# Output matmuls as four 32-row float32 strips, two batches at a time, in place of split fp32r products

## The chip, the cores and the metric

The kernel runs on one core of a Trainium2 chip. The metric is the device time of one execution in microseconds. The profiled execution is one execution of its own, recorded on the chip; its span is the time from its first to its last instruction.

## The reference

Three layers follow one another. Attention between 512 tokens and 32 state slots gives, for each of B = 8 batches, 544 rows of 512 numbers. A dense layer with a clipped square as its activation follows (w_in 512 x 2048, w_out 2048 x 512). The third layer is a soft mixture of experts, and the code that changes is its end:

```
logits = x @ phi                                  # 4352 tokens x 32 slots
d = softmax over tokens;  slot_input = d.T @ x    # 32 x 512
for e in range(8):                                # 4 slots per expert
    slot_out[e] = relu(slot_input[e] @ w1[e]) @ w2[e]
c = softmax over the 32 slots
out = c @ slot_out                                # 4352 x 32 times 32 x 512
```

Everything is float32. The output is 4352 x 512 numbers, 8.91 MB.

## The kernel before

The batches b = 0 to 7 (512 tokens each) and then one batch of the 256 state rows (b = B = 8) run through attention, the dense layer and the running softmax over tokens. What follows after that, in the profile from 455 us, is the tail. In it the slot inputs are multiplied by w1 (L906, sixteen slices of 1 MB), turned (L932) into `hTD`, and multiplied by w2 (L950, tile `SO`, again sixteen slices). All w1 and w2 slices are loaded by SyncE's queue (some by GpSimd's) as SBUF places come free (`give`, `take`, `free`).

The logits of every token lie in `LT` (and `LTs` for the state rows), transposed: 32t to 32t+31 are the 32 slots of the t-th 128 tokens of a batch, so `LT[32t:32t+32, 128b:128b+128]` is what the output matmul of 128 tokens needs as its stationary operand. `csoft` makes the softmax over slots in place, in VectorE and GpSimd, by way of the place `ct`.

The output matmul before the change works in fp32r, a float32 form whose matmul takes one record where float32 takes two. To keep the precision, each factor is split into a rounded part and the remainder. `csplit` brings the four strips of `LT` into one strip by multiplying with 0/1 matrices `pick` (tile `cX`), and writes rounded part and remainder under one another into `LC` (two batches per tile, `LCs` for the state rows). `slot_out(dh)` makes the slot outputs of one column half (dh = 0 or 1, 256 columns): eight steps of eight `SO` matmuls, one w2 slice each, then an eviction to `SOs`, a matmul with `R` that repeats the 32 rows four times (`SR`), and evictions into the four tiles `so`, whose unused rows are zeroed beforehand. `combine(dh)` makes the output of a column half: per 128 tokens two fp32r matmuls into `ops` (128x256), an eviction by VectorE or ScalarE in turn, and per batch one transfer of 512 KB from SyncE's queue. The state rows take eight transfers of 32 KB from GpSimd's queue per half.

Both are generators: the letters of `CFG["so"]` say whose turn it is, s for a step of `slot_out(1)`, c for a step of `combine(0)`. After that come what is left of both, and `combine(1)`. The build reorders instructions on an engine within their dependences, by a model of its own, so the order on an engine needn't be the order of the code.

```
    s1, c0 = slot_out(1), combine(0)
    for x in CFG["so"]:
        step(s1 if x == "s" else c0)
    drain(s1)
    drain(c0)
    drain(combine(1))
```

Of the kernel before, what the change touches and what calls it, by code (L numbers as in the profile page):

```python
# [7 lines left out]
F32 = mybir.dt.float32  # L8
# [8 lines left out]
CFG = dict(hp=2000, att7=(3, 5, 6, 7, 8, 10), og=1, n3=1, n3m=10, wS=['DP', 'AD', 'AD', 'AD', 'AD', 'DP', 'AD', 'DD', 'AD', 'AD', 'AD', 'AD', 'AD', 'AD', 'AD', 'AD'], xsm=13, k0=5, rg=6, spg=0, att0=6, att=7, V0=(2, 6, 10), Vn=(0, 4, 10), Vx=12, wn='H', wsev='adad', conv=(4, 8, 9, 11, 12, 13, 19, 21, 24, 26, 28, 32, 36, 40, 44, 48, 52, 56, 60), todo=[1, 1, 1, 2, 0, 0, 0, 3, 0, 0, 2, 2, 1, 1, 0, 0], E0=2, E=1, sm=1, tqB=(5, 9, 13), GP=10, pe=(3,), psH=3, gtpX=(0, 7), tq0=(13, 15), keep=(2, 3, 4, 5), x2=(1, 1), natm=1, warm=14, bounce7=(0, 3), split=1, wt=4, so='ssccsccccccsss', smm=(1, 2, 3, 4, 5, 6, 9), tqv=(), tqvm=0, first='x', apath=2, f32c=1, place=1, attm=(3, 6, 7, 8, 9, 12), subPm=True, loDm=False, bounce=(0, 1, 2, 3), bq=('s', 's'), xq='s', nat=((1, 11), (2, 2), (2, 3), (2, 11), (3, 2), (3, 4), (3, 9), (4, 2), (4, 3), (4, 9), (5, 2), (5, 3), (5, 9), (6, 2), (6, 4), (6, 9)), subP=(1,), mulD=(), loD=(), qlag=0, gv0='EEEEEEEEEEEEEEEE', gv='EEEEEEEEEEEEEEEE', gvS='BBBBBBBBBBBBBBBB')  # L17
# [3 lines left out]
def kernel(  # L21
# [657 lines left out]
    def csplit(parts, C):  # L679

        np_ = 64 * len(parts)
        X = psX.tile([128, 512], F32, tag="X", name="cX")[0:np_, 0:C.shape[1]]
        for q, (L, n) in enumerate(parts):
            for t in range(n // 128):
                mm(out=X[64 * q:64 * q + 64, 128 * t:128 * t + 128], lhsT=pick[0:n // 4, t, :], rhs=L, start=True, stop=True)
        act(C, X)
        for p in range(32, np_, 64):
            nc.vector.tensor_tensor(out=C[p:p + 32], in0=X[p:p + 32], in1=C[p:p + 32], op=ALU.subtract)

# [212 lines left out]
    for i in range(16):  # L902
        e, hf = divmod(i, 2)
        place, w = where["w1", i]
        for kt in range(4):
            mm(out=h1[hf][32 * kt:32 * kt + 32, :], lhsT=XD[e // 4][:, kt, 32 * (e % 4):32 * (e % 4) + 32], rhs=w[kt],  # L906
               start=(e == 0), stop=(e == 7))
        if i >= CFG["k0"] and len(place) == 1 and got < 4:
            got += 1
            kept.append(place)  # L910
        else:
            give(place)
# [3 lines left out]
    pick = tail4[:, 1, 0:2].rearrange("p a (b x) -> p (a b) x", b=2)  # L916
    for t in range(4):
        nc.vector.tensor_scalar(out=pick[:, t, :], in0=R[:, 0:64], scalar1=blk[:, t:t + 1], scalar2=None, op0=ALU.mult)
# [3 lines left out]
    LC = take(kept.pop(0), "LC", F32R)[1]  # L922
    LCs = const.tile([64, 256], F32R, tag="wp", name="LCs")
# [12 lines left out]
    so = take(kept.pop(0), "so", F32R)[1]  # L936
    for t in so:
        nc.vector.tensor_scalar(out=t.rearrange("p (a b) -> p a b", a=2),
                                in0=cst_t[:, 0:256].unsqueeze(1).to_broadcast([128, 2, 256]),
                                scalar1=0.0, scalar2=None, op0=ALU.mult)  # L940
    so = [so[0:2], so[2:4]]

    def slot_out(dh):
# [14 lines left out]
        for q in range(2):  # L958
            p, p2 = slice(64 * q, 64 * q + 64), slice(64 * q, 64 * q + 32)
            act(so[0][q][p, dc], SR[p])  # L960
            nc.vector.tensor_tensor(out=so[1][q][p2, dc], in0=SR[p2], in1=so[0][q][p2, dc], op=ALU.subtract)

    def combine(dh):
        dc = slice(256 * dh, 256 * dh + 256)
        n_ev = 0
        for b in list(range(B - 2)) + [B, B - 2, B - 1]:
            T = ntok(b) // 128
            place = next(p for p in free if p[0][2] >= 256 * T)
            free.remove(place)
            o = take(place, "o")[0][0][:, 0:256 * T].rearrange("p (t d) -> p t d", t=T)  # L970
            for t in range(T):
                q, p, L = (b % 2, slice(0, 128), LC[b // 2]) if b < B else (0, slice(0, 64), LCs)
                ps = (psH, psX)[n_ev % 2].tile([128, 256], F32, tag="HX"[n_ev % 2], name="ops")
                for i in range(2):
                    mm(out=ps, lhsT=L[p, 128 * t:128 * t + 128], rhs=so[i][q][p, dc], start=(i == 0), stop=(i == 1))  # L975
                if n_ev % 2:
                    act(o[:, t, :], ps)
                else:
                    nc.vector.tensor_copy(out=o[:, t, :], in_=ps)  # L979
                n_ev += 1  # L980
            if b < B:
                dma(out=out[544 * b:544 * b + 512, dc].rearrange("(t p) d -> p t d", p=128), in_=o)
            else:
                for bb in range(B):
                    t, q = divmod(bb, 4)
                    (nc.gpsimd.dma_start if CFG["og"] else dma)(out=out[544 * bb + 512:544 * bb + 544, dc], in_=o[32 * q:32 * q + 32, t, :])  # L986
# [4 lines left out]
    csplit([(LTs, NS)], LCs)  # L991
# [47 lines left out]
```

## Time and profile before

| | us |
|---|---|
| median of 3 runs | 539.94 |
| the runs | 536.88, 539.94, 543.04 |
| profiled execution: its span, the only time recorded of it | 537.7 |
| TensorE busy in it (matmul) | 481.8 (90%) |
| VectorE busy | 395.4 (74%) |
| ScalarE busy | 256.0 (48%) |
| GpSimd busy | 239.8 (45%) |

The share of TensorE is an average over stages with different limits; the rows further down keep the stages of the tail apart. DMA share is the mean busy share of the 16 DMA engines; about 1 means that they had no more to give.

### The profile page before, as it was taken

The page shows a single profiled execution, that of the slowest core. Times are in us where ns is not written, and L with a number is a line of the kernel's source. Part 1 is how long each engine was busy: PE and PEld are TensorE (multiplying, and loading weights), DVE is VectorE, ACT ScalarE, POOL GpSimd, SP SyncE. Part 2 cuts the span into 40 slices and gives each one's busy share as a digit, 9 for nine tenths or more (in the row PEclk, how much of TensorE's full clock was granted, in tenths as well). Part 3 has the DMA queues.
Part 4 walks back from the last instruction along what each step waited for, and adds up shares of the span by engine and source line. Part 5 has one row for each costly group of instructions (what it writes and reads, how often), then busy time and mean ns, then how long its engine had stood idle before and what let it go on. Part 6 is the DMA issues. An engine that isn't in the chain of part 4 may idle for free.

```text
span 537.7 us, 9910 instructions
## 1 busy us (share of the span) xinstructions
PE 481.8 (90%) x3757; PEld 273.0 (51%) x3757; DVE 395.4 (74%) x728; ACT 256.0 (48%) x508; POOL 239.8 (45%) x230
## 2 busy tenths in 40 slices
PE   4476999999987999999999999999997997999992
PEld 2132455665534555455455455456466683356481
DVE  2999989777578679969969979977964762345260
ACT  2343476576555456456455455455444462023152
POOL 0775667665317366465555555646471000110032
PEclk9686799999999999999999999999998999899996
DMA  8998082457378488789789878879797988996379
GB/s 314 419 402 325 1 293 100 157 177 197 117 227 322 110 296 289 240 251 276 283 219 274 276 222 265 285 221 349 260 324 217 364 338 306 388 419 249 118 254 294
DMA packets 40223, 140.30 MB, mean 261 GB/s; under 512 B 4336, under 2 KB 12912, under 8 KB 28272
## 3 DMA queue, kind: packets, MB, share of 16 engines
q1 hardware_dynamic: 38496, 131.81, 71.2%
q0 software_dynamic: 1680, 7.87, 4.4%
q8 instruction: 29, 0.48, 0.3%
q14 instruction: 18, 0.15, 0.1%
HBM read 98.24 MB, written 39.32 MB: 256 GB/s over the span
## 4 chain that ended last, share of the span: by engine, by line
PE 60%; DVE 18%; DMA 13%; ACT 3%; issue 2%; SPq 2%; POOL 0%; POOLq 0%; DVEq 0%; ACTq 0%
PE h L434 22%; PE F L123 5%; DMA gdr<-gD 4%; PE E L123 4%; PE V L123 4%; PE SO L950 4%; DMA nat<-gD 4%; PE h L442 4%; DMA nat<-gdr 3%; PE ops L975 3%; PE h L906 3%; DVE win L160 3%; PE gtp L512 2%; DVE win L158 2%; DVE v L384 2%
## 5 line engine op out<-in xcount | busy, mean ns | idle before, releaser
L434 PE MATMUL h<-a,v 128*128 128x512 f32 x744 | 200.3, 412 | 5.0 <-DVE nat L486 2.2
L464 POOL TENSOR_TENSOR c<-c 128x512 f32<-128x512 f32 x128 | 135.6, 1064 | 100.4 <-ACT c L132 99.9
L434 PEld LDWEIGHTS h<-a,v 128*128 128x128 f32 x744 | 133.9, 191 | 85.1 <-issue 28.2
L132 ACT ACTIVATE c<-h,half 128x512 f32<-128x512 f32 x128 | 87.8, 688 | 99.1 <-PE h L434 66.6
L486 DVE SCALAR_TENSOR_TENSOR g<-h,c 128x512 f32<-128x512 f32 x112 | 75.2, 672 | 29.8 <-POOL c L464 29.7
L521 DVE STREAM_TRANSPOSE gD<-g 128x512 f32<-128x512 f32 x108 | 75.6, 703 | 1.6
L132 ACT ACTIVATE v<-V 128x512 fp32r<-128x512 f32 x62 | 37.0, 597 | 29.5 <-DVE v L384 14.8
L384 DVE TENSOR_TENSOR v<-V,v 128x512 fp32r<-128x512 f32 x62 | 42.1, 679 | 10.5 <-ACT v L132 9.7
L123 PE MATMUL V<-win,st_t 64*32 64x512 f32 x64 | 35.1, 629 | 9.8 <-POOL win L168 6.5
L128 PE MATMUL V<-win,st_t 64*32 64x512 f32 x448 | 38.3, 630 | 0.0
L123 PE MATMUL F<-nat,dN 128*32 128x512 f32 x54 | 26.9, 601 | 4.5 <-DMA nat<-gdr 2.9
L123 PE MATMUL E<-g,wp 128*32 128x512 f32 x56 | 29.2, 604 | 0.7 <-DVE g L486 0.7
L128 PE MATMUL E<-g,wp 128*32 128x512 f32 x168 | 29.6, 604 | 0.0
L128 PE MATMUL F<-nat,dN 128*32 128x512 f32 x162 | 27.2, 601 | 0.0
L986 POOL DMA_DIRECT2D out_dram<-o x16 | 7.9, 501 | 42.8 <-DVE o L979 37.2
L442 PE MATMUL h<-XSh,v 128*128 128x256 f32 x128 | 26.4, 298 | 0.2 <-ACT nat L132 0.2
L979 DVE COPY o<-ops 128x256 f32<-128x256 f32 x34 | 13.6, 423 | 15.8 <-PE ops L975 15.4
L623 DVE SCALAR_TENSOR_TENSOR acc<-acc,al,F 128x512 f32<-128x512 f32 x28 | 20.7, 739 | 5.7 <-PE F L128 5.5
L320 POOL TENSOR_TENSOR a<-att,a 128x512 fp32r<-128x512 f32 x14 | 18.1, 1305 | 13.4 <-ACT a L132 13.4
L975 PE MATMUL ops<-so,LC 128*128 128x256 f32 x128 | 23.3, 308 | 0.2
L442 PEld LDWEIGHTS h<-XSh,v 128*128 128x128 f32 x128 | 21.2, 197 | 4.1 <-issue 1.9
L264 POOL TENSOR_TENSOR att<-att,m 128x512 f32<-128x512 f32 x14 | 15.1, 1081 | 18.3 <-DVE m L263 15.6
(239 smaller groups left out, 780.9 us busy)
## 6 DMA issues: line engine op xcount, KB each, us to landing
gdr<-gD SPq DMA_DIRECT2D x100, 256.0 KB, 4.8
nat<-gdr SPq DMA_DIRECT2D x25, 1024.0 KB, 5.5
w<-in_w_dram SPq DMA_DIRECT2D x24, 1024.0 KB, 8.8
xn<-in_xn_dram SPq DMA_DIRECT2D x8, 1024.0 KB, 7.7
out_dram<-o SPq DMA_DIRECT2D x16, 512.0 KB, 5.4
xs<-in_xs_dram SPq DMA_DIRECT2D x7, 1024.0 KB, 7.7
w<-in_w_dram POOLq DMA_DIRECT2D x5, 1024.0 KB, 9.5
wb<-in_win_dram SPq DMA_DIRECT2D x4, 1024.0 KB, 11.7
```

Of the source, the lines that this page charges most:

```text
L123: first = mm(**calls[0])
L128: e = mm(**c)
L132: return nc.scalar.activation(out=out, in_=in_, func=func, **kw)
L384: nc.vector.tensor_tensor(out=lo[:, G, :], in0=V[G], in1=hi[:, G, :], op=ALU.subtract)
L434: mm(out=h, lhsT=v[:, G, f], rhs=a[:, G, :], start=(k == 0), stop=(k == 5))
L442: mm(out=h, lhsT=w[:, j, :], rhs=x[:, j, :], start=(k == 0), stop=(k == 11))
L464: nc.gpsimd.tensor_tensor(out=c, in0=c, in1=c, op=ALU.mult)
L486: gI[b, m] = nc.vector.scalar_tensor_tensor(out=g, in0=h, scalar=1.0, in1=c, op0=ALU.max, op1=ALU.min)
L521: nc.vector.transpose(out=gd[:, :, :, m4, :].rearrange("p c a i -> p a c i"), in_=gT[b, m].rearrange("p (a c i) -> p a c i", a=4, i=32))
L623: nc.vector.scalar_tensor_tensor(out=a, in0=a, scalar=al, in1=F, op0=ALU.mult, op1=ALU.add)
L950: mm(out=SO[c:c + 32, :], lhsT=hTD[:, ft, 32 * e:32 * e + 32], rhs=w[ft // 2][:, 256 * (ft % 2):256 * (ft % 2) + 256], start=(e == 0 and f ...
L975: mm(out=ps, lhsT=L[p, 128 * t:128 * t + 128], rhs=so[i][q][p, dc], start=(i == 0), stop=(i == 1))
```

## The change

`csplit`, `pick`, `LC`, `LCs` and the zeroed `so` tiles are gone; two SBUF places fewer are set aside for them. `so` is now one float32 piece of the tile `tail` (128x512), which holds the 32 slot outputs four times under one another, as `SR` delivers them: one eviction of 128x256 per half. The output matmul takes strip t of `LT` as it lies, with 32 rows, and strip t of `so`, in float32. The helper `group` issues the matmuls of the four strips next to one another and keeps them together by a priority.

`combine` now goes through five groups per half: batches 0 and 1, then the state rows, then 2 and 3, 4 and 5, 6 and 7. Strip t has a PSUM bank of its own (`banks`): two banks of the pool V and two of X, or three of H and one of X, in turn. In a bank the two batches stand side by side, so that one eviction takes 128x512. The transfers per batch are those of before. `CFG["so"]` changes from `ssccsccccccsss` to `cscscscscssss`: each group of `combine(0)` is followed by one step of `slot_out(1)`, and four steps are left at the end.

```diff
...
-    def csplit(parts, C):
-
-        np_ = 64 * len(parts)
-        X = psX.tile([128, 512], F32, tag="X", name="cX")[0:np_, 0:C.shape[1]]
-        for q, (L, n) in enumerate(parts):
-            for t in range(n // 128):
-                mm(out=X[64 * q:64 * q + 64, 128 * t:128 * t + 128], lhsT=pick[0:n // 4, t, :], rhs=L, start=True, stop=True)
-        act(C, X)
-        for p in range(32, np_, 64):
-            nc.vector.tensor_tensor(out=C[p:p + 32], in0=X[p:p + 32], in1=C[p:p + 32], op=ALU.subtract)
-
...
         for kt in range(4):
             mm(out=h1[hf][32 * kt:32 * kt + 32, :], lhsT=XD[e // 4][:, kt, 32 * (e % 4):32 * (e % 4) + 32], rhs=w[kt],
                start=(e == 0), stop=(e == 7))
-        if i >= CFG["k0"] and len(place) == 1 and got < 4:
+        if i >= CFG["k0"] and len(place) == 1 and got < 2:
             got += 1
             kept.append(place)
         else:
...
 
     ct_place = kept.pop(0)
     ct, = take(ct_place, "ct")[0]
-    pick = tail4[:, 1, 0:2].rearrange("p a (b x) -> p (a b) x", b=2)
-    for t in range(4):
-        nc.vector.tensor_scalar(out=pick[:, t, :], in0=R[:, 0:64], scalar1=blk[:, t:t + 1], scalar2=None, op0=ALU.mult)
     csoft(LTs, 128, 64, SIs)
     csoft(LT, 128 * B, 128, ct)
     free.append(ct_place)
-    LC = take(kept.pop(0), "LC", F32R)[1]
-    LCs = const.tile([64, 256], F32R, tag="wp", name="LCs")
     hTD_t, = take(kept.pop(0), "hTD")[0]
...
-    so = take(kept.pop(0), "so", F32R)[1]
-    for t in so:
-        nc.vector.tensor_scalar(out=t.rearrange("p (a b) -> p a b", a=2),
-                                in0=cst_t[:, 0:256].unsqueeze(1).to_broadcast([128, 2, 256]),
-                                scalar1=0.0, scalar2=None, op0=ALU.mult)
-    so = [so[0:2], so[2:4]]
+    so = run["tail"][:, 512:1024]
 
     def slot_out(dh):
         dc = slice(256 * dh, 256 * dh + 256)
...
         act(SOs, SO)
         SR = psE.tile([128, 256], F32, tag="E", name="SR")
         mm(out=SR, lhsT=R, rhs=SOs, start=True, stop=True)
-        for q in range(2):
-            p, p2 = slice(64 * q, 64 * q + 64), slice(64 * q, 64 * q + 32)
-            act(so[0][q][p, dc], SR[p])
-            nc.vector.tensor_tensor(out=so[1][q][p2, dc], in0=SR[p2], in1=so[0][q][p2, dc], op=ALU.subtract)
+        act(so[:, dc], SR)
+
+    def banks(n):
+
+        V = psV.tile([128, 2, 512], F32, tag="V", name="oV")
+        return [V[:, 0], V[:, 1]] + [psX.tile([128, 512], F32, tag="X", name="oX") for _ in range(2)] if n % 2 == 0 else [
+            psH.tile([128, 512], F32, tag="H", name="oH") for _ in range(3)] + [psX.tile([128, 512], F32, tag="X", name="oX")]
 
     def combine(dh):
+
         dc = slice(256 * dh, 256 * dh + 256)
         n_ev = 0
-        for b in list(range(B - 2)) + [B, B - 2, B - 1]:
-            T = ntok(b) // 128
-            place = next(p for p in free if p[0][2] >= 256 * T)
+        for n, bs in enumerate([(0, 1), (B,), (2, 3), (4, 5), (6, 7)]):
+            T, nb = ntok(bs[0]) // 128, len(bs)
+            place = next(p for p in free if p[0][2] >= 256 * T * nb)
             free.remove(place)
-            o = take(place, "o")[0][0][:, 0:256 * T].rearrange("p (t d) -> p t d", t=T)
+            o = take(place, "o")[0][0][:, 0:256 * T * nb].rearrange("p (t b d) -> p t b d", t=T, b=nb)
+            ps = banks(n)[0:T]
+            group([dict(out=ps[t][:, 256 * i:256 * i + 256],
+                        lhsT=(LT[32 * t:32 * t + 32, 128 * b:128 * b + 128] if b < B else LTs[32 * t:32 * t + 32, :]),
+                        rhs=so[32 * t:32 * t + 32, dc], start=True, stop=True)
+                   for i, b in enumerate(bs) for t in range(T)])
             for t in range(T):
-                q, p, L = (b % 2, slice(0, 128), LC[b // 2]) if b < B else (0, slice(0, 64), LCs)
-                ps = (psH, psX)[n_ev % 2].tile([128, 256], F32, tag="HX"[n_ev % 2], name="ops")
-                for i in range(2):
-                    mm(out=ps, lhsT=L[p, 128 * t:128 * t + 128], rhs=so[i][q][p, dc], start=(i == 0), stop=(i == 1))
+                v = ps[t][:, 0:256 * nb].rearrange("p (b d) -> p b d", b=nb)
                 if n_ev % 2:
-                    act(o[:, t, :], ps)
+                    act(o[:, t], v)
                 else:
-                    nc.vector.tensor_copy(out=o[:, t, :], in_=ps)
+                    nc.vector.tensor_copy(out=o[:, t], in_=v)
                 n_ev += 1
-            if b < B:
-                dma(out=out[544 * b:544 * b + 512, dc].rearrange("(t p) d -> p t d", p=128), in_=o)
-            else:
-                for bb in range(B):
-                    t, q = divmod(bb, 4)
-                    (nc.gpsimd.dma_start if CFG["og"] else dma)(out=out[544 * bb + 512:544 * bb + 544, dc], in_=o[32 * q:32 * q + 32, t, :])
+            for i, b in enumerate(bs):
+                if b < B:
+                    dma(out=out[544 * b:544 * b + 512, dc].rearrange("(t p) d -> p t d", p=128), in_=o[:, :, i])
+                else:
+                    for bb in range(B):
+                        t, q = divmod(bb, 4)
+                        (nc.gpsimd.dma_start if CFG["og"] else dma)(out=out[544 * bb + 512:544 * bb + 544, dc], in_=o[32 * q:32 * q + 32, t, 0])
             free.append(place)
             yield
 
     drain(slot_out(0))
-    csplit([(LTs, NS)], LCs)
-    for i in range(NL):
-        csplit([(LT[:, 128 * b:128 * b + 128], 512) for b in range(2 * i, min(2 * i + 2, B))], LC[i])
     s1, c0 = slot_out(1), combine(0)
```

TensorE, from the last `SO` step of the first column half (w_7) to the first steps of the second half (w_8, w_9 and on); `cX` is `csplit`, `ops` the output matmul. Before:

```order
L950 MATMUL SO<-w_7_4507,hTD 32x256 x8
L685 MATMUL cX<-LT,tail 64x128 x16
L957 MATMUL SR<-tail,cst_t 128x256
L685 MATMUL cX<-LT,tail 64x128 x8
L975 MATMUL ops<-so,LC 128x256 x2
L685 MATMUL cX<-LT,tail 64x128 x8
L975 MATMUL ops<-so,LC 128x256 x5
L950 MATMUL SO<-w_8_4513,hTD 32x256 x8
L950 MATMUL SO<-w_9_4519,hTD 32x256 x8
L975 MATMUL ops<-so,LC 128x256 x3
L950 MATMUL SO<-w_10_4525,hTD 32x256
```

After; `oV`, `oX`, `oH` are the banks of the output matmul:

```order
L929 MATMUL SO<-w_7_4507,hTD 32x256 x8
L936 MATMUL SR<-tail,cst_t 128x256
L123 MATMUL oV<-tail,LT 128x256
L128 MATMUL oV<-tail,LT 128x256
L128 MATMUL oX<-tail,LT 128x256 x2
L128 MATMUL oV<-tail,LT 128x256 x2
L128 MATMUL oX<-tail,LT 128x256 x2
L929 MATMUL SO<-w_8_4513,hTD 32x256 x8
L123 MATMUL oH<-tail,LTs 128x256
L128 MATMUL oH<-tail,LTs 128x256
L929 MATMUL SO<-w_9_4519,hTD 32x256 x8
```

The 32 `cX` matmuls between the last `SO` step and `SR`, and behind it, are gone. A first group of eight float32 output matmuls (`oV`, `oX`) follows `SR` at once, and the `SO` steps stand whole between groups, where before output matmuls cut them into pieces from w_10 on.

TensorE again, from the second `SR` on, to the end of the program before:

```order
L957 MATMUL SR<-tail,cst_t 128x256
L975 MATMUL ops<-so,LC 128x256 x4
L975 MATMUL ops<-so,LCs 128x256 x2
L975 MATMUL ops<-so,LC 128x256 x44
L975 MATMUL ops<-so,LCs 128x256 x2
L975 MATMUL ops<-so,LC 128x256 x20
L975 MATMUL ops<-so,LCs 128x256 x2
L975 MATMUL ops<-so,LC 128x256 x8
```

After, the first twelve rows from the second `SR` on:

```order
L936 MATMUL SR<-tail,cst_t 128x256
L123 MATMUL oV<-tail,LT 128x256
L128 MATMUL oV<-tail,LT 128x256
L128 MATMUL oX<-tail,LT 128x256 x2
L128 MATMUL oV<-tail,LT 128x256 x2
L128 MATMUL oX<-tail,LT 128x256 x2
L123 MATMUL oH<-tail,LTs 128x256
L128 MATMUL oH<-tail,LTs 128x256
L123 MATMUL oH<-tail,LT 128x256
L128 MATMUL oH<-tail,LT 128x256
L123 MATMUL oV<-tail,LT 128x256
L128 MATMUL oV<-tail,LT 128x256
```

In place of 68 fp32r matmuls of the second half, and what was left of the first, stand 34 float32 ones. The first group is whole; of the next, a part of batches 4 and 5 (`oH`) is taken ahead of batches 2 and 3 (`oV`, `oX`).

ScalarE, from the eviction of the first `SO` half on. Before:

```order
L132 ACTIVATE tail<-SO 128x256
L132 ACTIVATE LC<-cX 128x512 x2
L132 ACTIVATE so<-SR 64x256
L132 ACTIVATE LC<-cX 128x512
L132 ACTIVATE so<-SR 64x256
L132 ACTIVATE LC<-cX 128x512
L132 ACTIVATE o<-ops 128x256 x9
```

After:

```order
L132 ACTIVATE tail<-SO 128x256
L132 ACTIVATE tail<-SR 128x256
L132 ACTIVATE o<-oV 128x512
L132 ACTIVATE o<-oX 128x512
L132 ACTIVATE o<-oH 128x256
L132 ACTIVATE o<-oV 128x512
L132 ACTIVATE o<-oX 128x512
```

The four evictions into `LC` and the second one into `so` are gone, and the output evictions each take a bank of two batches (128x512), but for that of the state rows (`oH`, 128x256).

## Rows read from the trace of the kernel before

**Rows 1.** Busy time by stage: us, engines' busy us (instructions), granted clock, DMA share.

```profile
core 0: us, PE busy (x) PEld busy (x) DVE busy (x) ACT busy (x) POOL busy (x), PEclk, DMA share, GB/s
455.00:491.20 36.20, 34.38 (x365) 17.47 (x357) 14.46 (x29) 7.05 (x15) 4.11 (x3) 0.95 1.01 408
491.20:516.00 24.80, 24.80 (x203) 13.26 (x201) 10.09 (x23) 6.02 (x16) 2.04 (x4) 1.00 0.32 105
516.00:536.00 20.00, 11.74 (x77) 9.81 (x76) 7.38 (x19) 8.65 (x24) 5.87 (x12) 0.82 1.03 330
536.10:537.70 1.60, 0.00 (x0) 0.00 (x0) 0.00 (x0) 0.00 (x0) 0.00 (x0) 0.50 0.04 14
```

**Rows 2.** The chain that ended last, tail, in order of time: start us, us, what.

```profile
477.44 0.58 PE cX L685 x4
478.01 7.06 PE SO L950 x128
485.07 1.53 PE cX L685 x19
...
492.29 0.78 PE ops L975 x5
...
501.10 0.56 PE SO L950 x6
501.66 0.43 PE ops L975 x2
...
514.69 0.43 PE SR L957 x2
```

**Rows 3.** SyncE's queue from 480 us on, its waits: us in all, times, longest.

```profile
SPq L982 <- ACT o L132: 28.6, 15, 4.5
```

**Rows 4.** Timeline of the tail: start us, us, engine, line, operation, shapes.

```profile
470.27 1.55 DVE L938 TENSOR_SCALAR so<-cst_t 128x512 fp32r<-128x512 f32 x4
...
477.52 0.38 ACT L132 ACTIVATE hTD<-hTp 128x256 f32<-128x256 f32 x1 [1.29 <-PE hTp L932]
...
485.20 0.38 ACT L132 ACTIVATE tail<-SO 128x256 f32<-128x256 f32 x1 [6.77 <-PE SO L950]
...
488.24 0.38 ACT L132 ACTIVATE so<-SR 64x256 fp32r<-64x256 f32 x1
...
496.91 33.55 SPq L982 DMA_DIRECT2D out_dram<-o  x16
```

**Rows 5.** Groups by line and shape: busy us, mean ns, idle before.

```profile
L621 DVE COPY acc<-F 128x512 f32<-128x512 f32 x4 | 2.8, 689 | 3.0 <-PE F L128 3.0
```

**Rows 6.** Timeline of TensorE and its weight loads around one V group.

```profile
212.50 0.66 PE L128 MATMUL V<-win,st_t 64*32 64x512 f32 x7
...
212.52 0.16 PEld L128 LDWEIGHTS V<-win,st_t 64*32 64x32 f32 x11
...
212.95 0.63 PE L128 MATMUL V<-win,st_t 64*32 64x512 f32 x7
...
213.51 1.66 PE L434 MATMUL h<-a,v 128*128 128x512 f32 x6
```

**Rows 7.** Timeline of TensorE's weight loads, `hTp`.

```profile
475.46 1.86 PEld L932 LDWEIGHTS hTp<-cst_t,tail 128*128 128x128 f32 x16 [0.84 <-ACT tail L132]
```

**Rows 8.** Timeline of TensorE, output matmuls of the second half.

```profile
515.95 5.97 PE L975 MATMUL ops<-so,LC 128*128 128x256 f32 x44
```

**Rows 9.** Page, part 6: DMA issues, KB each, median us to landing.

```profile
out_dram<-o SPq DMA_DIRECT2D x16, 512.0 KB, 5.4
...
out_dram<-o POOLq DMA_DIRECT2D x16, 32.0 KB, 4.7
```

**Rows 10.** Stretches of 2 us in the output stage.

```profile
518.00:520.00 2.00, 2.00 (x18) 1.96 (x17) 1.71 (x6) 1.25 (x4) 0.69 (x2) 1.00 0.91 248
...
522.00:524.00 2.00, 2.00 (x16) 1.87 (x17) 1.71 (x5) 0.88 (x3) 0.89 (x2) 1.00 1.06 358
...
526.00:528.00 2.00, 1.80 (x8) 1.09 (x8) 0.00 (x0) 1.53 (x4) 1.27 (x3) 1.00 1.01 296
```

More of the change, by code (lines that the diff above doesn't have):

```diff
@@ L14 @@
 PSUM = bass.MemoryType.PSUM
-CFG = dict(hp=2000, att7=(3, 5, 6, 7, 8, 10), og=1, n3=1, n3m=10, wS=['DP', 'AD', 'AD', 'AD', 'AD', 'DP', 'AD', 'DD', 'AD', 'AD', 'AD', 'AD', 'AD', 'AD', 'AD', 'AD'], xsm=13, k0=5, rg=6, spg=0, att0=6, att=7, V0=(2, 6, 10), Vn=(0, 4, 10), Vx=12, wn='H', wsev='adad', conv=(4, 8, 9, 11, 12, 13, 19, 21, 24, 26, 28, 32, 36, 40, 44, 48, 52, 56, 60), todo=[1, 1, 1, 2, 0, 0, 0, 3, 0, 0, 2, 2, 1, 1, 0, 0], E0=2, E=1, sm=1, tqB=(5, 9, 13), GP=10, pe=(3,), psH=3, gtpX=(0, 7), tq0=(13, 15), keep=(2, 3, 4, 5), x2=(1, 1), natm=1, warm=14, bounce7=(0, 3), split=1, wt=4, so='ssccsccccccsss', smm=(1, 2, 3, 4, 5, 6, 9), tqv=(), tqvm=0, first='x', apath=2, f32c=1, place=1, attm=(3, 6, 7, 8, 9, 12), subPm=True, loDm=False, bounce=(0, 1, 2, 3), bq=('s', 's'), xq='s', nat=((1, 11), (2, 2), (2, 3), (2, 11), (3, 2), (3, 4), (3, 9), (4, 2), (4, 3), (4, 9), (5, 2), (5, 3), (5, 9), (6, 2), (6, 4), (6, 9)), subP=(1,), mulD=(), loD=(), qlag=0, gv0='EEEEEEEEEEEEEEEE', gv='EEEEEEEEEEEEEEEE', gvS='BBBBBBBBBBBBBBBB')
+CFG = dict(hp=2000, att7=(3, 5, 6, 7, 8, 10), og=1, n3=1, n3m=10, wS=['DP', 'AD', 'AD', 'AD', 'AD', 'DP', 'AD', 'DD', 'AD', 'AD', 'AD', 'AD', 'AD', 'AD', 'AD', 'AD'], xsm=13, k0=5, rg=6, spg=0, att0=6, att=7, V0=(2, 6, 10), Vn=(0, 4, 10), Vx=12, wn='H', wsev='adad', conv=(4, 8, 9, 11, 12, 13, 19, 21, 24, 26, 28, 32, 36, 40, 44, 48, 52, 56, 60), todo=[1, 1, 1, 2, 0, 0, 0, 3, 0, 0, 2, 2, 1, 1, 0, 0], E0=2, E=1, sm=1, tqB=(5, 9, 13), GP=10, pe=(3,), psH=3, gtpX=(0, 7), tq0=(13, 15), keep=(2, 3, 4, 5), x2=(1, 1), natm=1, warm=14, bounce7=(0, 3), split=1, wt=4, so='cscscscscssss', smm=(1, 2, 3, 4, 5, 6, 9), tqv=(), tqvm=0, first='x', apath=2, f32c=1, place=1, attm=(3, 6, 7, 8, 9, 12), subPm=True, loDm=False, bounce=(0, 1, 2, 3), bq=('s', 's'), xq='s', nat=((1, 11), (2, 2), (2, 3), (2, 11), (3, 2), (3, 4), (3, 9), (4, 2), (4, 3), (4, 9), (5, 2), (5, 3), (5, 9), (6, 2), (6, 4), (6, 9)), subP=(1,), mulD=(), loD=(), qlag=0, gv0='EEEEEEEEEEEEEEEE', gv='EEEEEEEEEEEEEEEE', gvS='BBBBBBBBBBBBBBBB')
 @with_exitstack
```

## The prediction, made before the changed kernel ran

> **What bounds the kernel now.** I read first the busy time by stage after 455 us, where the code that the diff touches begins [rows 1]. Three stages show themselves. Until 491.2 us the DMA engines are full (share 1.01, 408 GB/s): the weights w1 and w2 are coming in. From 491.2 to 516 they are nearly empty (0.32, 105 GB/s), while TensorE is busy for all of the 24.8 us. From 516 to 536 they are full again (1.03, 330 GB/s): now the output goes out. After 536.1 only 1.6 us of closing work is left. So in the middle stage the transfer that will end the kernel is not running because TensorE hasn't made the output yet; that is 24.8 x (1 - 0.32) = 16.9 us of idle DMA.
>
> Second, the chain of waits says what TensorE does meanwhile [rows 2]. The first column half of the slot outputs (`SO`) ends at 485.07. Then come the matmuls of `csplit` (`cX`) in three batches, with ScalarE and VectorE splitting `LC` between them, and from 492 on the output matmuls (`ops`) and the second `SO` half take turns, 0.56 and 0.43 us a turn; `SR` of the second half comes only at 514.69. Third, SyncE's queue: it waits 15 times for evictions by ScalarE, 28.6 us in all [rows 3], and its first output transfer is issued at 496.91 [rows 4].
>
> **The change, part by part.** All sums are made against the profiled execution: its span of 537.7 us is the only time it has, 0.4% under the median of 539.94; at the end I scale by that ratio.
>
> *Taken away before the first half.* `pick` (four small VectorE instructions) and the zeroing of `so` (1.55 us on VectorE) lie beside the w1 matmuls, and the `csplit` of `LTs` (0.58 us of TensorE) stands while ScalarE makes `hTD`, for which the first `SO` matmul waits anyway [rows 2, 4]. I cost these at nothing: the start of `SO` stays at 478.0 and its end at 485.1. Their cover is the w1 stage and the `hTD` eviction; without it the two that have rows would be worth 2.1 us. The two SBUF places that are kept no longer shift three w2 loads to other places, but the loads run at full DMA share already, so I keep their end at 491.2.
>
> *From `SO` to the first output transfer.* Before: 485.07 to 496.91, 11.8 us. After: eviction of `SO` (starts 0.13 after, takes 0.38), `SR` 0.43, eviction into `so` 0.38 [rows 2, 4], with the small gaps 486.5. Then one group of eight matmuls, which I call G, and two 128x512 evictions in a row on each of VectorE and ScalarE (0.689 us on VectorE in the nearest row, also a copy from PSUM to SBUF [rows 5]), 1.4 us.
>
> *What is G?* No row shows four row strips. One matmul of 128x256 in full float32 takes 0.43 (`SR`, two records of 0.213). Eight of them one after another would be 3.4 us; in two rounds of four side by side 0.85. The nearest row is the group that makes V: two row strips times four column strips, eight matmuls of 512 columns, whose second round of eight records starts 0.45 us after the first [rows 6]; a lone matmul takes that per record too (two records in 0.43 at half the columns). So the strips there cost nothing extra, and their weight loads also run together: eleven within 0.16 us. What differs here is that a weight load is 128 columns wide: sixteen such loads in a row took 1.86 us, 0.116 each [rows 7], which bounds G from above if loads of different strips have to go one by one. Ends: 0.85 and 3.4; I take 1.0 (0.85 and one load of 0.12), by the V group, which shares the trait in question, row strips.
>
> The Trainium skill, "TensorE: Matmul & The Clock Gate", section "Part 3: Packing small matmuls — row/col tiling", speaks against that: a weight load overlaps a running matmul only where the row groups differ. By it the four records in one strip would each pay their load, G would be 4 x (0.116 + 0.213) = 1.3 us, an estimate from the rows, and the second half's output would come just as the DMA engines run dry: the sum below would hold, the reserve in it would be gone. The trace doesn't bear the rule out: six full-height matmuls of 512 columns took 1.66 us, 0.27 each [rows 6], less than a load and a stream end to end.
>
> *The two halves, TensorE.* Eight `SO` steps are 7.06 us, as in the first half, since they now stand whole; before, they were cut into pieces. The turns also show the price of changing between the two forms: 0.43 for two output matmuls that take 5.97/44 = 0.136 each in a row [rows 8], and 0.56 for 0.44: together 0.28 us per round trip. Five round trips: 1.4 us. The first half's groups: four G and one of a quarter (the summary slots, two matmuls) = 4.25 G. So `SO` ends at 486.5 + 4.25 G + 7.1 + 1.4 = 495.0 + 4.25 G, and 1.4 (SO eviction, SR, so) + G + 1.4 (evictions) later the first output of the second half can be issued: 497.8 + 5.25 G; with G = 1.0, 503.1.
>
> *Evictions.* 34 of 128x256 a half become 16 of 128x512 and two of 128x256, half of them on VectorE: under 9 x 0.69 = 6.2 us per half. A group's are 1.4 us; its transfer is over 3 us (below). They hide behind the DMA. Without that cover they would cost under 12.4 us for both halves.
>
> *The output transfers.* Number, size and order on SyncE and GpSimd are as before, apart from the summary slots, which go second and no longer third from last: 16 of 512 KB and 16 of 32 KB, 8.91 MB [rows 9]. They stand in SyncE's queue behind the loads; the first is issued at 486.5 + 1.0 + 1.4 = 488.9, before these end at 491.2, so nothing is lost between the two. At 330 GB/s, the mean of 516 to 536, 8.91 MB take 27.0 us. Half of it is out at 491.2 + 13.5 = 504.7; the second half begins to come at 503.1, and from there a group per 1.4 us meets a transfer of 3.2 us per group. So the DMA engines don't run dry: 491.2 + 27.0 = 518.2, and 1.6 for the end: **519.8 us**. The other way round: 537.7 - 16.9 = 520.8, if exactly the idle time goes. The bound after the change is the output transfer itself, and that is what is late next. Times 539.94/537.7: **522 us**. Bounds: single 2 us stretches of the output stage went at 358 and at 296 GB/s [rows 10], which gives 24.9 and 30.1 us, spans of 517.7 and 522.9.
>
> **The rivals.**
> - *The second half comes late.* If weight loads of the strips go one by one (G = 1.86) or two strips at a time run (1.7), the second half comes at 507.6 or 506.7, and the DMA engines stand idle for 2 to 2.9 us: span 521.8 to 522.7, and with the slower transfer rate 525.8: 524 to 528 us. For it speaks rows 7, against it the loads of the V group. The limit is G = 1.3.
> - *No strips side by side at all.* G = 3.4: the last group ends at 486.5 + 7.1 + 1.4 + 1.4 + 8.5 x 3.4 = 525.3, then 0.7 of eviction, 5.4 to landing [rows 9], 1.6: 533.0, as a median 535. TensorE is then the bound again. Against it: the V group.
> - *Slower.* One after another, and every weight load in full view, because a strip's load can't go under its own stream: G = 16 x (0.116 + 0.213) = 5.3, last group at 541.5, span 549, median 551. It decides from G = 3.9 up. The pitch of 0.27 in rows 6 speaks against it.
> - *The output writes are slow by themselves.* From 518 to 520 they went at 248 GB/s, at a DMA share of 0.91 [rows 10]. If this is what small transfers from GpSimd do to the others, and they now stand in the middle of each half, 8.91 MB take up to 36 us: span 528.7, median 531.
> - *It doesn't do what it says*: the scheduler takes the groups apart. The order of TensorE shows whole groups in the first half, and pieces of groups in the second, which has TensorE time to spare; then 537 to 540.
>
> **How the numbers follow.** Within 1% is about what a measurement of this kernel can tell from no change: the three runs lie 0.6% about their median. The forecast, DMA full to the end, 518 to 524: 0.64. The second half late, 524 to 528: 0.18. Slow writes, 526 to 531: 0.06. Serial strips, 535: 0.05. Not as written, 537 to 540: 0.03. Slower, 551: 0.04. Faster by over 1% is below 534.5: 0.64 + 0.18 + 0.06 = 0.88; within 1%: 0.08; slower: 0.04. For the range, the low end is the fast transfer rate, 517.7 x 1.004 = 519.9, less 0.6% of spread between runs: 517. The high end takes in the second half late and half of the slow writes: 529. About 0.15 is left out.
>
> **What would show it.** In the profile after, the DMA share stays near 1.0 from 455 to about 518, with no stretch of 2 us under 0.8. SyncE's first output issue is near 489 and the second half's first one near 503. A group of eight matmuls shows its second round of records in each strip about 0.2 us after the first and lasts about 1 us; at 1.8 or 3.4 one of the rivals holds. `SO` steps take 0.9 us each, undivided. The chain of waits ends with output transfers, not with TensorE. I am wrong if the output evictions wait for TensorE after 505, if the loads end later than 491, or if the stretch before 478 moves, which the order of instructions gives no cause for.

## The result, and the profile after

The changed kernel takes **521.09 us** (median of 4 runs, 519.87 to 522.32) where the kernel before takes 539.15 (4 runs, 536.88 to 543.04): a ratio of 0.9667, 95% interval 0.9623 to 0.9711. The forecast was 522, in a range of 517 to 529. The profiled execution is the longest of the four: its span is 520.2, its time 522.32. (Of the experiments below, one profiled execution of the doubled groups took 1125 us, twice as long from its first stage on; nothing is read from it, and it and the longest runs of e3 and e11 stand in the medians but not in the ratios.)

Busy time by stage, after; the columns are those of [rows 1], and so is the first stage:

```profile
core 0: us, PE busy (x) PEld busy (x) DVE busy (x) ACT busy (x) POOL busy (x), PEclk, DMA share, GB/s
455.00:491.20 36.20, 33.45 (x374) 15.20 (x370) 10.27 (x18) 6.06 (x13) 5.55 (x6) 0.95 1.00 407
491.20:516.00 24.80, 15.93 (x198) 10.03 (x190) 9.17 (x15) 8.64 (x17) 6.45 (x14) 0.89 1.00 332
516.00:518.20 2.20, 0.00 (x0) 0.00 (x0) 0.00 (x0) 0.00 (x0) 0.00 (x0) 0.50 1.03 344
518.20:520.20 2.00, 0.00 (x0) 0.00 (x0) 0.00 (x0) 0.00 (x0) 0.00 (x0) 0.50 0.08 27
```

The middle stage carried 105 GB/s before and carries 332 now. The third stage of before, 20 us of output at full share, has shrunk to 2.2 us, and the close is 2.0. TensorE, busy for all of the middle stage before, now has 9 of its 24.8 us free. So the DMA engines are full from 455 to 518, but for a dip that is told further down, and end the kernel.

The chain of waits in the tail, after, in order of time, answers to [rows 2]: start us, us, what.

```profile
477.37 7.16 PE SO L929 x128
484.53 0.02 issue
...
485.05 0.71 PE SR L936 x2
...
486.22 0.48 PE oV L123
...
487.37 1.00 PE SO L929 x16
488.37 0.41 PE oH L123
...
495.67 3.63 PE SO L929 x64
...
499.77 0.71 PE SR L936 x2
```

No `cX` stands between the first half of `SO` and the output; the `SO` steps of the second half stand whole, 16 records at a time, in 1.00 us, and the last four together in 3.63. `SR` of the second half starts at 499.77, 14.9 us earlier than in [rows 2].

The first group and its evictions, from the timeline: start us, us, engine, line, operation, shapes, and in brackets the idle time ahead and who ended it.

```profile
486.22 0.48 PE L123 MATMUL oV<-tail,LT 32*128 32x256 f32 x1 [0.47 <-ACT tail L132]
...
486.24 0.48 PE L128 MATMUL oX<-tail,LT 32*128 32x256 f32 x2
486.33 0.18 PEld L123 LDWEIGHTS oV<-tail,LT 32*128 32x128 f32 x1
...
486.54 0.37 PE L123 MATMUL oV<-tail,LT 32*128 32x256 f32 x1
...
486.76 0.38 PE L128 MATMUL oV<-tail,LT 32*128 32x256 f32 x2
...
486.98 0.38 PE L128 MATMUL oV<-tail,LT 32*128 32x256 f32 x2
...
487.30 1.07 PE L929 MATMUL SO<-w,hTD 128*32 128x256 f32 x16
487.40 0.69 DVE L964 COPY o<-oV 128x512 f32<-128x512 f32 x1 [10.07 <-PE oX L128]
...
488.13 0.60 ACT L132 ACTIVATE o<-oV 128x512 f32<-128x512 f32 x1 [1.96 <-DVE o L964]
...
489.24 0.95 SPq L968 DMA_DIRECT2D out_dram<-o  x2
```

Four strips start within 0.02 us of each other (486.22 and 486.24 are two of them), and each strip's later records follow at 0.32, 0.22 and 0.22. The group ends, where the chain goes over to `SO`, at 487.37: G = 1.15. The load at 486.33 runs while the matmul of 486.22 in its own strip still streams. The last two rows but one show what I had not seen: ScalarE starts its copy 0.73 us after VectorE started its own, 0.04 after VectorE ended (487.40 + 0.69 = 488.09), and the bracket names VectorE. The first output transfer goes out at 489.24.

### The profile page after: what moved, and what is told of

Its sections match the earlier page's. It is cut to its first block, busy times and chain, and to the rows that moved or that the text cites. A ratio compares the mean times of both kernels' runs of the same rounds, so it can differ in the third digit from the quotient of the medians.

```text
span 520.2 us, 9680 instructions
## 1 busy us (share of the span) xinstructions
PE 458.6 (88%) x3689; PEld 258.5 (50%) x3689; DVE 384.9 (74%) x691; ACT 248.6 (48%) x485; POOL 237.4 (46%) x230
## 4 chain that ended last, share of the span: by engine, by line
PE 49%; DVE 23%; DMA 14%; ACT 5%; issue 2%; SPq 2%; POOL 2%; DVEq 0%; ACTq 0%
PE h L434 17%; DMA gdr<-gD 5%; PE F L123 5%; DMA nat<-gD 4%; DMA nat<-gdr 4%; PE E L123 4%; PE h L442 4%; PE h L895 3%; PE V L123 3%; PE SO L929 3%; DVE win L158 2%; DVE win L160 2%; DVE gD L521 2%; DVE v L384 2%; DVE g L486 2%
## 5 line engine op out<-in xcount | busy, mean ns | idle before, releaser
L434 PE MATMUL h<-a,v 128*128 128x512 f32 x744 | 198.1, 408 | 6.3 <-DVE nat L486 3.5
L123 PE MATMUL V<-win,st_t 64*32 64x512 f32 x64 | 34.2, 615 | 10.5 <-POOL win L168 7.1
L128 PE MATMUL V<-win,st_t 64*32 64x512 f32 x448 | 37.1, 614 | 0.0
L286 POOL TENSOR_TENSOR att<-att,z 128x512 f32<-128x512 f32 x16 | 17.4, 1087 | 10.0 <-DVE z L285 6.8
L168 POOL TENSOR_TENSOR win<-win,LT 128x512 uint32<-128x512 uint32 x7 | 10.9, 1568 | 22.3 <-DVE win L160 14.8
```

What stands on the lines that cost most here:

```text
L123: first = mm(**calls[0])
L128: e = mm(**c)
L286: (nc.vector if b in CFG["mulD"] else nc.gpsimd).tensor_tensor(out=t3, in0=t3, in1=z1.unsqueeze(2).to_broadcast([128, 16, 32]), op=ALU.mult)
L434: mm(out=h, lhsT=v[:, G, f], rhs=a[:, G, :], start=(k == 0), stop=(k == 5))
```

## The experiments

All ratios are to the kernel before, run beside the experiment on the same chip. The profiled executions reach the tail at different times (the first `SO` matmul starts between 476.7 and 482.1 us), so where stages are compared I count from that start to the end of the span, called **tail** below: 59.7 us before (537.7 less 478.01), 42.8 after (520.2 less 477.37). The difference, 16.9, is what the prediction had found as idle DMA time.

**Where the 18 us come from: e1, e2, e3, e12, e4.** My theory: the split of `LT` (`csplit`) and the shape of the output matmuls each hold TensorE up, and the order of turns alone (the string `so`) gives little.

*e1, the order of turns alone, in the kernel before.*
```
-so='ssccsccccccsss'
+so='cscscscscssss'
```


> The kernel before, with the turn letters of the changed one (c, s, c, s ...). If the gain came from the order of turns, this alone gives most of it: a span of 520 to 528. If it came from the work that TensorE no longer does, the same matmuls stand in another order and the second SR comes no earlier than 514: span 536 to 539, and the time is that of before within 1%.

Measured: 537.43, ratio 0.9951 (0.9913 to 0.9989); tail 57.2, second `SR` at 511.83. The turns alone are worth about 2.5 us of 18; `SR` came 2 us earlier than I had expected.

*e2, the kernel before without `csplit`.*
```
-    drain(slot_out(0))
-    csplit([(LTs, NS)], LCs)
-    for i in range(NL):
-        csplit([(LT[:, 128 * b:128 * b + 128], 512) for b in range(2 * i, min(2 * i + 2, B))], LC[i])
+    for c, s in [(LCs, cst_t[0:64, 0:256])] + [(c, LT[:, 0:512]) for c in LC]:
+        nc.vector.tensor_scalar(out=c, in0=s, scalar1=1.0, scalar2=None, op0=ALU.mult)
+    drain(slot_out(0))
```


> The kernel before, in which csplit is left out: LC and LCs are filled by one VectorE copy each, so the output is not the reference's. If the split alone held the output back, the whole gain comes here: span about 520. By the working of the prediction only the stretch from the end of the first SO half to the first turns (485.1 to 493.1, with 1.4 of SR left in it) goes, some 6 to 6.5 us: span 531 to 532, and the turns of fp32r matmuls and SO pieces hold the rest.

Measured: 530.76, ratio 0.9832 (0.9765 to 0.99); tail 50.2, which is 9.5 shorter than before's. The middle stage, e2:

```profile
491.20:516.00 24.80, 24.77 (x228) 16.63 (x228) 11.87 (x31) 9.03 (x25) 4.01 (x8) 1.00 0.70 239
```

TensorE is still busy in all of it (24.77 of 24.80), and the DMA share is only 0.70. So without the split TensorE remains the bound.

*e3, the changed kernel with `csplit` put back, its result unused* (with it come back its definition, `pick`, `LC`, `LCs` and the two SBUF places; left out here).
```
...
+    csplit([(LTs, NS)], LCs)
+    for i in range(NL):
+        csplit([(LT[:, 128 * b:128 * b + 128], 512) for b in range(2 * i, min(2 * i + 2, B))], LC[i])
     s1, c0 = slot_out(1), combine(0)
```


> The changed kernel with csplit done as before, its result unused. If the split's 6 us of TensorE are on the path of the second half, the first output of that half moves from 504 to about 510, the DMA engines stand idle 5 to 6 us more, and the span is 524 to 527. If the DMA engines' time alone counts (the split hides behind the transfers), it stays at 520 to 521.

Measured: 536.24, ratio 0.9939 (0.991 to 0.9968), tail 57.3: nearly all of the gain gone, and far over what both theories expected. The chain of waits, e3:

```profile
493.68 1.06 PE oX L128 x4
...
498.80 1.06 PE oX L128 x4
...
503.32 1.06 PE oX L128 x4
...
504.94 1.06 PE oX L128 x4
```

`csplit` takes its banks from the pool of `oX`, so a group finds one `oX` late, and its one strip runs by itself: 1.06 us for a quarter of a group that takes 1.15 whole. There are six such pieces between 493.68 and 510.19. The run measures the split and broken groups together.

*e12, the same as e3, with `cX` in the pool of `oH`.*
```
-        X = psX.tile([128, 512], F32, tag="X", name="cX")
+        X = psH.tile([128, 512], F32, tag="H", name="cX")
```


> The changed kernel with csplit added back, its result unused, and its tile in the H banks and no longer in the X banks, so that the groups of output matmuls stay whole. If the other run with the split lost 15 us because the split costs some 6 to 7 us and the broken groups the rest, this one loses only the first part: the second SR moves from 499.8 to 505 to 507, and the span is 525 to 528. If the split costs 15 us by itself, 534 to 536.

Measured: 528.27, ratio 0.9783 (0.9746 to 0.982); tail 48.6, 5.8 more than after's; second `SR` at 505.88. Not all of this is the split. In e12 the first half of `SO` takes 8.73 us, in the changed kernel 7.16 for the same matmuls, and the granted clock is lower at its start. The row of the chain, and the stretch, with the clock ahead of the DMA share:

```profile
477.51 8.73 PE SO L945 x128
...
478.00:480.00 2.00, 2.00 (x24) 0.92 (x20) 0.00 (x0) 0.00 (x0) 0.00 (x0) 0.50 1.02 426
```

In the changed kernel the granted clock is 1.00 from the start of this `SO` half to its end. So 1.57 us of e12's tail are the clock, not the split; that `SR` came at 505.88, where it was expected, is in part luck. Two rows of its timeline show what remains: the first batches of `cX`, and VectorE's half of the splitting.

```profile
486.17 2.57 PE L685 MATMUL cX<-LT,pk 128*64 128x128 f32 x32
...
488.42 2.82 DVE L688 TENSOR_TENSOR LC<-cX,LC 32x512 fp32r<-32x512 f32 x4 [10.99 <-ACT LC L132]
```

So by the traces the split costs the changed kernel 4.2 us (5.8 less 1.6), and the kernel before 9.5; whether the other runs of e12 had the lower clock at the same place, no trace shows. The rest of e3's loss (57.3 less 47.0, 10.3 us) goes with the pool: the six pieces in its chain are 6.4 us of it, the rest is not taken apart here.

*e4, the changed kernel with the order of turns of before.*
```
-so='cscscscscssss'
+so='ssccsccccccsss'
```


> The changed kernel with the turn letters of before (s, s, c, c, s ...). Two SO steps ahead of the first group move the first output by 1.8 us, to 491.0, just to the end of the loads; the second half comes at the same time, since TensorE has the same work ahead of it. Span 520 to 521.5. If the order of turns made the gain, 525 or more.

Measured: 523.58, ratio 0.9731 (0.9684 to 0.9778), tail 44.4. First output at 490.70, as expected; second `SR` at 501.21, counted from the start of `SO` 1.8 us later than in the changed kernel, where I had expected no difference. The turns are worth 1.6 us of tail here, 2.5 in e1.

**What a group costs: e5 and e11, e6, e13, e10, e7.** My theory: strips run side by side and their weight loads are hidden. The rivals: loads serialize within a strip (G = 1.3) or across strips (1.86), or strips don't run side by side at all (3.4, and 5.3 with every load in full view).

*e5, and again as e11: every group twice.*
```
-                   for i, b in enumerate(bs) for t in range(T)])
+                   for i, b in enumerate(bs) for t in range(T)] * 2)
```


> The changed kernel with every group of output matmuls issued twice (the second pass writes the same numbers again). A group lasts about 2.0 us in place of the 1.15 measured. If the prediction's sum for the second half holds (5.25 groups ahead of its first transfer), that transfer moves from 504.0 by 4.5 us to 508.4, the DMA engines stand idle about 4 us longer and the span is 523.5 to 525. If only the DMA engines' work counts, 520 to 521.

> The same as the run with doubled groups, whose profiled execution was disturbed, for a profile: a group of about 2.0 us, the second half's first transfer at 508 to 509, the DMA engines short of work by about 4 us between 503 and 509, span 523.5 to 525.

Measured: 529.12 and 528.61, ratios 0.9754 (0.9681 to 0.9828) and 0.9757 (0.9687 to 0.9827). In the trace of e11 the first group lasts from 490.95 to 492.96, 2.0 us, 0.86 more than once. With 8.5 groups in both halves that adds 7.3 us to TensorE; by the two ratios (0.009 over the change's own) 4.8 of it reaches the end, by the tail of this trace (530.0 less 482.10, 47.9) 5.1, by the spans (524.9 as the mean of the six shorter runs, 519.0 as that of the change's four) 5.9. The intervals of the ratios just overlap the change's own, so the size is rough. The second half's first transfer goes out at 513.43, counted from the start of `SO` 4.7 later than in the changed kernel; 4.5 was expected. The output's DMA time hides only the rest.

*e6, the records of a strip one behind the other in the program.*
```
-                   for i, b in enumerate(bs) for t in range(T)])
+                   for t in range(T) for i, b in enumerate(bs)])
```


> The changed kernel with the matmuls of a group in another order: both batches of strip 0, then of strip 1, and so on, so that neighbours in the queue want the same strip. If four strips side by side are what makes a group cheap, a group goes from 1.15 to 2.8 to 3.4 us; the second half's first output then comes at 512 to 516 and TensorE ends the kernel: span 528 to 534. If strips make no difference, 520 to 521.

Measured: 522.6, ratio 0.9661 (0.9609 to 0.9713), span 520.9: no difference to the change, and a clear miss. I had taken it that TensorE starts matmuls in the order of the program. TensorE, first group of e6:

```profile
487.12 0.48 PE L123 MATMUL oV<-tail,LT 32*128 32x256 f32 x1 [0.47 <-ACT tail L132]
487.14 0.48 PE L128 MATMUL oV<-tail,LT 32*128 32x256 f32 x1
487.15 0.49 PE L128 MATMUL oX<-tail,LT 32*128 32x256 f32 x2
487.44 0.37 PE L123 MATMUL oV<-tail,LT 32*128 32x256 f32 x1
...
487.66 0.39 PE L128 MATMUL oV<-tail,LT 32*128 32x256 f32 x2
...
488.22 0.64 PE L929 MATMUL SO<-w,hTD 128*32 128x256 f32 x8
```

In the program four `oV` matmuls, strip 0 and then strip 1, stand ahead of the four `oX` of strips 2 and 3, and the build leaves them in that order. The trace has `oX` start at 487.15, 0.03 after the first `oV`; the strips' later records, those of the second matmul of strip 0 among them, follow at 487.44 and 487.66. The group takes 488.22 - 487.12 = 1.10; counted the same way it takes 487.30 - 486.22 = 1.08 in the changed kernel. So this order within a group makes no difference, and the rivals on loads can't be told apart by it.

*e13, two strips instead of four.*
```
-    lhsT=(LT[32 * t:32 * t + 32, ...]), rhs=so[32 * t:32 * t + 32, dc]
+    lhsT=(LT[32 * (t % 2):32 * (t % 2) + 32, ...]), rhs=so[32 * (t % 2):32 * (t % 2) + 32, dc]
```


> The changed kernel with the output matmuls on two strips in place of four (t modulo 2), the rest kept; the output isn't the reference's. On one strip the granted clock fell to 0.50 and the span rose to 564. If the price of a group goes by the strips that run side by side and the clock holds at 1.00, a group takes 1.9 to 2.2 us, the second half's first transfer comes at 508 to 509.5, and the span is 523 to 526. If two strips aren't enough to hold the clock either, groups take 3.6 us and more, the SO steps double too, and the span is 540 or more.

Measured: 527.12, ratio 0.9773 (0.9727 to 0.9819); first group 485.61 to 487.60, G = 1.99, and the granted clock stays at 1.00 until 512; the second half's first transfer goes out at 506.94, earlier than I had expected, and in 502 to 508 the DMA share is 0.50. That is the rival "the second half comes late", brought about by the edit: it had put G = 1.7 to 1.86 at 524 to 528.

*e10, one strip for all.*
```
-    lhsT=(LT[32 * t:32 * t + 32, ...]), rhs=so[32 * t:32 * t + 32, dc]
+    lhsT=(LT[0:32, ...]), rhs=so[0:32, dc]
```


> The changed kernel with all output matmuls on strip 0 (LT and so from rows 0 to 31 for every t), so that nothing runs side by side; the number, shape and order of the instructions are kept, the output isn't the reference's. If strips side by side make a group cheap, a group goes from 1.15 to 3.5 to 4.2 us (in the run with the split added, two matmuls alone on one strip took 1.06): TensorE becomes the bound again, the second half's first output comes at 516 to 520, and the span is 531 to 538, near the kernel before. If the form of the matmul doesn't matter as long as the split is gone, 520 to 523.

Measured: 561.7, ratio 1.0423 (1.0371 to 1.0475), far beyond what I expected. Stretches of e10; the column to read is the granted clock, ahead of the DMA share:

```profile
486.00:488.00 2.00, 1.14 (x4) 0.71 (x5) 0.00 (x0) 0.71 (x2) 0.00 (x0) 1.00 1.00 410
488.00:490.00 2.00, 2.00 (x8) 1.55 (x7) 0.00 (x0) 0.00 (x0) 0.00 (x0) 0.61 1.02 426
490.00:492.00 2.00, 2.00 (x7) 1.50 (x6) 0.00 (x0) 0.00 (x0) 0.00 (x0) 0.50 1.01 422
...
500.00:510.00 10.00, 10.00 (x36) 6.47 (x36) 1.38 (x2) 1.19 (x2) 1.66 (x4) 0.50 0.24 74
...
530.00:535.00 5.00, 4.01 (x26) 2.75 (x19) 0.00 (x0) 0.77 (x2) 0.00 (x0) 1.00 0.02 3
535.00:536.00 1.00, 1.00 (x6) 0.85 (x5) 0.78 (x2) 0.06 (x1) 0.00 (x0) 1.00 0.00 0
```

The group begins at 487.56 at a granted clock of 1.00; in the next stretches it is 0.61 and then 0.50, that is 1.2 instead of 2.4 GHz, although TensorE is busy without a gap. It is back at 1.00 by the stretch from 530, after TensorE had turned from the groups to the last four `SO` steps (from 524.73 on). The second half's groups begin at 532.33, and the clock falls again, to 0.62 in the stretch from 536 to 537 and 0.50 after that. The chain of waits, e10, first half and second:

```profile
487.56 0.69 PE oV L123 x2
488.25 0.53 PE oV L128 x2
488.78 1.71 PE oX L128 x4
...
493.90 1.86 PE SO L929 x16
...
532.33 0.69 PE oV L123 x2
...
533.46 0.86 PE oX L128 x4
...
535.18 0.86 PE oX L128 x4
536.04 0.54 PE oH L123 x2
```

The first group takes 6.3 us, and an `SO` step that takes 1.00 in the changed kernel takes 1.86, at the same work. The second half's first group, 532.33 to 536.04, runs before the clock falls: 3.71 us at a granted clock of 1.00, within the 3.5 to 4.2 expected. Its records follow at 0.86/4 = 0.215, the pitch of `SR`'s two [rows 2], so the loads of one strip, 0.116 each [rows 7], hide under that strip's own stream. This tells the rivals on loads apart: every load in full view (G = 5.3) is excluded, and so is a load ahead of each record of a strip (G = 1.3), since both want a pitch of 0.33. Loads one by one across the strips (1.86) are excluded by G = 1.15. With G = 3.71 the prediction's own sum for serial strips gives a span of 535.6, an estimate; the spans of e10 are 559.4 to 564.1, so some 24 to 28 us are the clock.

*e7, one b in each group.*
```
-[(0, 1), (B,), (2, 3), (4, 5), (6, 7)]
+[(0,), (1,), (B,), (2,), (3,), (4,), (5,), (6,), (7,)]
```
and with it `so='ccscsccsccsccssss'`.

> The changed kernel with one batch per group and 128x256 evictions, as many groups as batches. A group of four is about 0.65 us, two of them 1.3 and more changes between the two forms of matmul: the second half 2 to 3 us later, span 521.5 to 523.5. If pairing two batches carries the gain, 526 or more.

Measured: 524.76, ratio 0.9714 (0.9657 to 0.977), spans 521.4 to 524.4, as expected on the whole. The first output goes out at 487.47, 1.8 us earlier, while the loads still fill the DMA engines; the second half's first one at 505.95, 2.0 later, and from 502 to 508 the DMA share is 0.47.

**What is left: e9, evictions divided by banks, and one more group ahead of the second `SR`.**
```
-                if n_ev % 2:
+                if (t // 2 if n % 2 == 0 else n_ev % 2):
```
and with it `so='cscscsscsssss'`.

> The changed kernel with two things mended: in groups on V and X, VectorE evicts both V banks and ScalarE both X banks, so that ScalarE doesn't wait for VectorE; and the last group of the first half stands in the gap before the second SR. The second half's first transfer then comes at 502 to 503 in place of 504, and the dip of the DMA engines between 502 and 508 (about 0.9 us of idle time) shrinks or goes: span 519 to 520. No gain if the dip has another cause.

Measured: 522.23, ratio 0.9661 (0.9618 to 0.9705): no difference to the change in time. Its timeline, the first group's evictions:

```profile
488.25 1.29 DVE L964 COPY o<-oV 128x512 f32<-128x512 f32 x2 [10.06 <-PE oX L128]
488.29 1.08 ACT L132 ACTIVATE o<-oX 128x512 f32<-128x512 f32 x2 [1.28 <-PE oX L128]
```

The two engines now start 0.04 us apart. So what ScalarE had waited for was VectorE's copy from the other bank of the same tile `oV`: with both banks of `oV` on one engine that wait is gone. The second half's first transfer goes out at 503.56, counted from the start of `SO` 1.2 us earlier than in the changed kernel. The stretches of 502 to 508 hold 1.04 to 1.05 and 1.02 of DMA share, so the dip that the changed kernel has there is gone too; a smaller one stands ahead of it, 0.88 from 500 to 502. The tail is 41.9 against 42.8 us, a difference that the timed runs don't confirm.

## Why the prediction was right, point by point

**The bound.** Right. TensorE kept the output back and the DMA engines now end the kernel. 8.91 MB in 27.0 us, at 330 GB/s, was the term that set the time, and 491.2 to 518.2 is what they took. That it fits so closely is in part luck: outside the dip the rate was higher, 361 GB/s from 491.2 to 502 and 343 from 508 to 518.2, and the dip took back what that gained. The close took 2.0 instead of 1.6, so the span is 520.2 instead of 519.8.

**Taken away before the first half, costed at nothing.** Right as far as the profile tells: `SO` starts at 477.37 against 478.0, and the w1 stage itself starts 0.6 earlier (459.28 against 459.88), so the removal of the `LTs` split and of the zeroing shows nothing of its own.

**The two causes.** Counted on TensorE from the first `SO` matmul to the second `SR`: 36.7 us before, 27.9 in e2 (no split), 26.8 in e12 (new form, with split; 28.4 less the 1.6 of the clock), 22.4 after. The split is worth 8.8 or 4.4, the form of the matmuls and the order of turns together 9.9 or 5.5, by which of them goes first; together 14.3 of the tail's 16.9. The turns alone are 3.8 of this by e1 (32.9) and 1.8 by e4 (24.2). Within the form: from the first output matmul to the second `SR`, e2's chain has 9.4 us of `ops` and 9.6 of `SO` in pieces, the changed kernel 5.45 of groups and 7.63 of `SO`. So between these two, which also differ in the order of turns, the groups take 4 us less in the first half, and the whole steps 2 less.

**The terms.**
- From `SO` to the first group: predicted 1.4, measured 484.53 to 486.22, 1.7; `SR`, put at 0.43, takes 0.71 now that it stands alone.
- G: predicted 1.0, measured 1.15. By the Trainium skill, "TensorE: Matmul & The Clock Gate", section "Part 3: Packing small matmuls — row/col tiling", a load overlaps a running matmul only where the row groups differ; the load at 486.33, in the strip that streams, does not agree, and neither does the pitch of 0.215 in one strip (e10). The same section also lets a load go ahead into a background weight buffer, and that would agree with these rows. Of the three gaps between a strip's records the first (0.32) is 0.10 over the others, which is near the 0.116 of a load [rows 7]; the other two (0.22) are those of `SR`'s two records and leave no room for one. At most one load of the four shows. The 0.27 that the prediction set against the rule [rows 6] is the pitch of fp32r matmuls (`v` and `a` are fp32r tiles), so it was weak evidence for the float32 ones; e10's rows are the evidence.
- The groups of the first half: predicted 4.25 G = 4.25, measured 5.45, because G is larger and the fourth group takes 1.50 (492.08 to 493.58), its `oX` part coming after the rest.
- Round trips between the forms: predicted 1.4 beside 7.1 of `SO`, measured 7.63 in all. With the first half of `SO` ending 0.5 earlier (484.53 against 485.07) the errors cancel, which is luck: the end of the second half of `SO` was put at 499.25 and is at 499.31.
- **Evictions: mis-sized.** Predicted 1.4 a group, measured 1.8 (487.40 to 489.22), since ScalarE waits for VectorE. From 484 to 500 that happens three times; the 6.5 us in this row are all of ScalarE's idle time ahead of the three copies, of which the wait for VectorE's copy is 0.73 to 0.79 each:

```profile
ACT o L132 <- DVE o L964: 6.5, 3, 2.3
```

"From there a group per 1.4 us" fails by the same cause. In the second half the groups on the V banks start at 500.94, 503.50 and 506.05, 2.55 apart, because the next one waits for ScalarE to free the bank; that is still below the 3.2 us of a group's transfer, and groups on the H banks come between.
- The first output: predicted 488.9, measured 489.24. The first of the second half: predicted 503.1, measured 503.96, since the way from `SO` to a group (1.6 here), G and the evictions each come in once more:

```profile
503.96 10.41 SPq L968 DMA_DIRECT2D out_dram<-o  x8
```

**The point that failed: "no stretch of 2 us under 0.8".** Stretches of 2 us, after:

```profile
502.00:504.00 2.00, 1.86 (x19) 1.33 (x16) 1.88 (x4) 1.15 (x3) 0.00 (x0) 1.00 0.93 312
504.00:506.00 2.00, 1.50 (x21) 1.07 (x18) 1.66 (x4) 0.81 (x3) 1.97 (x5) 1.00 0.68 215
506.00:508.00 2.00, 1.61 (x16) 1.15 (x16) 1.33 (x3) 1.02 (x3) 1.94 (x4) 1.00 0.94 274
```

They fall short of a full share by 0.07, 0.32 and 0.06, 0.9 us in all. The reserve that I had put at 504.7 - 503.1 = 1.6 us went from both ends: the second half's first transfer came 0.9 later, and the first half's were done sooner, since the DMA engines ran at 354 GB/s from 491.2 to 503.96 and not at 330. It cost at most those 0.9 us of a span that came out 0.4 over the forecast; e9, without the dip, is not measurably faster. Two signs of being wrong that the prediction had named also came, by the letter: after 505 evictions wait for TensorE (VectorE 0.67 us ahead of 507.23, ScalarE 1.22 ahead of 510.25), and the stretch before 478 moved by 0.6. Neither touched the bound: from 508 to 518.2 the DMA share is 1.04, and the 0.6 is small beside the 18 us.

**The rivals.** "The second half comes late" lies in the same chain and is near: G = 1.99 in e13 makes it true. "Serial strips" (3.4) is excluded by G, and e10 shows what they take, 3.71. "Slow writes" is excluded: the summary slots' small transfers now go out second in each half, and the middle stage still holds 332 GB/s. "Not as written" did not happen in the changed kernel, but e3 shows how near it lies: a tile in the wrong pool is enough. "Slower" is what one strip gives, yet by a cause that I did not have: not loads in full view (G = 3.71 at a clock of 1.00), but the granted clock.

## What to carry to other kernels

Where a stage at the end has its transfers waiting for an engine, the idle share of the DMA engines in it (here 16.9 us) was both the size of the gain and its limit; what made the engine still shorter than the transfer gained nothing more (e9). Small matmuls set side by side need all of their PSUM banks free at the same time, so count who else takes banks of those pools; and where evictions stand on the path, try both banks of a tile on one engine: in e9 the wait between the two engines was gone, though the time did not change.

## What the runs showed of the hardware that was not expected

- Eight float32 matmuls of 32 rows by 256 columns take 1.15 us in four row strips, 1.99 in two and 3.71 in one (e10, second half), at a granted clock of 1.00. In one strip the records follow at 0.215 us, so the weight loads don't show.
- With all of them in one strip (e10) the granted clock fell from 1.00 to 0.50 during the first group, with TensorE busy throughout, and stayed there through the full-height `SO` steps in between; it rose during the last four of them, and fell again in the second half's second group. Two strips (e13) kept 1.00 until 512, when only the last four records were left. No run tells why.
- Matmuls of different row strips start out of the program's order: `oX` at 487.15 in e6, ahead of an `oV` matmul that stands before it and starts at 487.66. The Trainium skill, "TensorE: Matmul & The Clock Gate", section "Part 3: Packing small matmuls — row/col tiling", says that matmuls start and end strictly in order; these rows don't agree with it for different strips.
